# A pause in the weight loads, a later zeroing and a new spacing of transposes in a fused attention and FFN kernel

## The chip, the cores and the metric

One core of a Trainium2 chip. The metric is the device time of one execution in microseconds (us), of which smaller is better. Fast: no more than 1.5% above the fastest of its kernel. "Ratio" is always the mean time of one kernel's fast runs over the mean of the other kernel's fast runs of the same rounds on the same chip, so it is not quite the ratio of the medians quoted beside it. The 95% interval is in brackets.

## The reference

Linear attention with cosine and sine features, followed by a multiplicative feed-forward part, in float32:

```python
# q, k, v: (8 batches, 8 heads, 576 positions, 64)
def phi(x, c, s):
    r = np.maximum(x, 0.0)
    return np.concatenate([r * c, r * s], axis=-1)        # 128 features
q_p, k_p = phi(q, cos_w, sin_w), phi(k, cos_w, sin_w)
kv  = np.einsum('bhsf,bhsd->bhfd', k_p, v)
z   = np.sum(k_p, axis=2)
num = np.einsum('bhsf,bhfd->bhsd', q_p, kv)
den = np.einsum('bhsf,bhf->bhs', q_p, z)[..., None] + 1e-06
x   = (num / den).transpose(0, 2, 1, 3).reshape(4608, 512)
out = ((x @ w1) * (x @ w2) @ w3) @ w_out                   # w1, w2: 512x1024; w3: 1024x1024; w_out: 1024x512
```

## The kernel before

The kernel works on nine tiles of 512 tokens. It multiplies w3 by w_out once (the "w34" work, which needs w3 transposed) and then spends its time in the products with w1, w2 and w34. Attention of the next batches is woven in between: units of work are appended to numbered "slots", and after each group of FFN matmuls the units of its slot are issued, each to its engine's own in-order stream. So the order in a slot list is the order on every engine.

All weights and most inputs are loaded by GpSimd, in one long list that is issued at the start:

```python
for c0, n in ((0, 256), (256, 256), (512, 256), (768, 256)):
    nc.gpsimd.dma_start(out=w1b[:, :, ds(c0, n)], in_=w1v[:, :, ds(c0, n)])
    nc.gpsimd.dma_start(out=w2b[:, :, ds(c0, n)], in_=w2v[:, :, ds(c0, n)])
    if c0 == 256:
        load_first4(nc.gpsimd, q0, q)
nc.gpsimd.dma_start(out=woutb[:], in_=moe_w_out.rearrange("(c p) m -> p c m", p=P))
for jp in range(8):
    load_w3(jp)
    if jp == 4:
        load(1, "k")
load(1, "qv")
load(2, "kqv")
```

The feature buffers exist twice, for even and odd batches. The second set is zeroed by VectorE in mid-kernel:

```python
def feature_buffers(i):
    va = const.tile([P, NCH, H, D + 2], BF16, name=f"va{i}")
    nc.vector.memset(va[:, :, :, D:D + 1], 1.0)
    nc.vector.memset(va[64:128, 4, :, 0:D], 0.0)
    ...                                       # cut: kp and qp, one memset each
```

One chunk of attention is a query transpose (TensorE, then a copy out of PSUM), a numerator (TensorE, then a normalisation on VectorE), and a transpose of the normalised block into xT, the FFN's input:

```python
def q_tr(b, c, evac=True):
    ...                                       # cut: 8 transposes into pst
    on_vector = lambda: nc.vector.tensor_copy(out=dst, in_=src)
    ...
def num(b, c, chain=True):
    nt = ps_att.tile([P, 2, 512], FP32, name="pnum")      # this pool has one buffer
    ...                                       # cut: 8 matmuls, then den, reciprocal, xblk on VectorE
def x_tr(b, c, by_vector=False):
    ...                                       # cut: 4 transposes of xblk into pst
    copy = nc.vector.tensor_copy if by_vector else nc.scalar.copy
    copy(out=xT[t][:, :, ds(o, R)], in_=pst[:, 0:4, 0:R])
```

Where they stand during the first token tile:

```python
slots[6].append(lambda: feature_buffers(1))
slots[6].append(lambda: prep_q(0, 4))
slots[8].append(lambda: q_tr(0, 4))
...
spread(prep_units(1, (prep_k,)), 8, 10, between)
spread(prep_units(1, (prep_q,)), 10, 13, between)
spread(prep_units(1, (prep_v,)), 13, 14, between)
attention_at(1, between, kv=(14, 14, 14, 15, 15), tr=(12, 13, 15, 17, 19),
             nu=(16, 17, 19, 20, 22), xt=(18, 19, 21, 22, 25))
...
spread(prep_units(2, (prep_k,)), 20, 23, slots)   # key features of batch 2: VectorE and ScalarE
```

## Time and profile before

| | before |
|---|---|
| three first runs | 260.17 us median (259.86 to 260.18) |
| span of the profiled execution | 258.3 us |
| TensorE busy | 247.0 us, 96% |
| idle time of TensorE with a named engine behind it | 4.7 us, all before 62 us |

The lines that carry this stand in the prediction below. One more stretch matters for what follows: the end of the first token tile, just before the second tile's first FFN matmul (L428). Timeline columns: start, duration, engine, line, operation, output from input, and in brackets the idle time before it with what ended it.

```profile
63.70 0.59 ACT L369 COPY xT<-pst 128x512 bf16<-128x512 bf16 x1
64.10 0.39 PE L367 MATMUL pst<-identb,xblk 128*128 128x128 bf16 x4
64.17 0.73 ACT L245 ACTIVATE kp<-ks,sinv 128x512 bf16<-128x512 bf16 x1
64.33 0.42 PE L331 MATMUL pnum<-kvs,qpT 128*128 128x65 bf16 x8
64.59 1.02 PE L474 MATMUL ffnps<-w34b,abT 128*128 128x512 bf16 x4
64.80 0.58 ACT L369 COPY xT<-pst 128x512 bf16<-128x512 bf16 x1
65.45 0.81 PE L428 MATMUL ffnps<-xT,w1b 128*128 128x512 bf16 x3
```

Read them engine by engine. ScalarE finishes the last copy into xT at 64.80 + 0.58 = 65.38 us, and TensorE starts the tile that reads it at 65.45: the two are level, TensorE has no idle time there, and its list of waits does not name this place. Nothing stands in reserve either.

### The profile page before, as it was taken

Reading aid. Unit: us, or ns where it says so; the run is one execution under the profiler, and the core shown is the slowest. Engines: PE = TensorE matmul, PEld = TensorE weight load, DVE = VectorE, ACT = ScalarE, POOL = GpSimd, SP = SyncE. Lnnn points to the kernel's source line nnn. Section 1 sums busy time; section 2 is a strip of 40 time slices with the busy share of each in tenths; the row PEclk is TensorE's granted clock in tenths of the full one; section 3 lists DMA queues with packets and bytes.
Section 4 is the critical chain, followed back from the end, with each engine's and each line's share of the span. In section 5 each row is a group of like instructions: output and inputs, shape, how many; then the busy total and the mean of one; then the engine's idle time right before and its main releaser. Section 6 shows DMA issues by size and latency. Waiting matters only on the chain.

```text
span 258.3 us, 5051 instructions
## 1 busy us (share of the span) xinstructions
PE 247.0 (96%) x1934; PEld 134.9 (52%) x1967; DVE 145.6 (56%) x346; ACT 127.9 (49%) x219; POOL 85.6 (33%) x146
## 2 busy tenths in 40 slices
PE   8889899999999999999999999999999999999992
PEld 3478455665565455446454654555455544444441
DVE  6875753856879638833972688178526614303310
ACT  2765224936965555545655465646533233323321
POOL 7854154440670384047305900610140031022000
PEclk9999999999999999999999999999999999999999
DMA  7999999999899599999998999826490252024025
GB/s 191 183 194 202 208 205 201 199 198 199 212 157 146 100 202 175 160 162 176 195 158 173 175 198 133 175 60 122 92 202 13 50 121 76 0 42 122 1 45 120
DMA packets 68025, 37.11 MB, mean 144 GB/s; under 512 B 35616, under 2 KB 64544, under 8 KB 68000
## 3 DMA queue, kind: packets, MB, share of 16 engines
q0 software_dynamic: 35488, 27.20, 65.6%
q1 hardware_dynamic: 32352, 9.44, 22.3%
q8 instruction: 15, 0.25, 0.4%
q10 hardware_dynamic: 160, 0.13, 0.2%
q14 instruction: 10, 0.08, 0.1%
HBM read 38.80 MB, written 9.44 MB: 187 GB/s over the span
## 4 chain that ended last, share of the span: by engine, by line
PE 89%; DMA 3%; DVE 2%; issue 2%; ACT 1%; POOL 1%; ACTq 0%; POOLq 0%
PE ffnps L428 47%; PE ffnps L474 23%; PE ffnps L208 5%; PE pnum L331 4%; PE pst L304 4%; PE pnum L273 3%; DMA qs<-in_q_dram 3%; PE pst L196 1%; PE pst L367 1%; DVE xblk L341 1%; DVE qp L241 0%; POOL vs L120 0%; ACT qpT L307 0%; PE ffnps L491 0%; ACT asb L465 0%
## 5 line engine op out<-in xcount | busy, mean ns | idle before, releaser
L469 DVE TENSOR_TENSOR abT<-asb,ffnps 128x512 bf16<-128x512 bf16 x68 | 46.4, 682 | 65.1 <-PE ffnps L428 64.1
L428 PE MATMUL ffnps<-xT,w1b 128*128 128x512 bf16 (+2 forms) x312 | 74.2, 357 | 0.8 <-DVE xT L369 0.3
L428 PE MATMUL ffnps<-xT,w2b 128*128 128x512 bf16 (+2 forms) x306 | 73.2, 356 | 0.5
L465 ACT CAST asb<-ffnps 128x512 bf16<-128x512 f32 x68 | 39.8, 585 | 63.9 <-PE ffnps L428 56.5
L474 PE MATMUL ffnps<-w34b,abT 128*128 128x512 bf16 x273 | 63.4, 379 | 0.4
L413 POOL DMA_DIRECT2D out_dram<-osb x42 | 22.3, 536 | 121.0 <-ACT osb L480 120.9
L428 PEld LDWEIGHTS <-w1b 128*128 128x128 bf16 x320 | 28.9, 98 | 27.2 <-issue 0.4
L474 PEld LDWEIGHTS <-abT 128*128 128x128 bf16 x280 | 26.5, 98 | 30.1 <-DVE abT L469 0.4
L480 ACT COPY osb<-ffnps 128x512 f32<-128x512 f32 x35 | 20.5, 585 | 38.6 <-PE ffnps L474 37.5
L428 PEld LDWEIGHTS <-w2b 128*128 128x128 bf16 x320 | 27.4, 97 | 22.7
L245 ACT ACTIVATE qp<-qs,sinv 128x512 bf16<-128x512 bf16 (+2 forms) x40 | 28.2, 717 | 1.2 <-DMA qs<-in_q_dram 1.2
L341 DVE TENSOR_TENSOR xblk<-pnum,den 128x512 bf16<-128x512 f32 (+1 forms) x39 | 26.9, 691 | 1.5 <-DVE den L340 0.2
L245 ACT ACTIVATE kp<-ks,sinv 128x512 bf16<-128x512 bf16 (+1 forms) x35 | 24.9, 722 | 0.0
L331 PEld LDWEIGHTS <-qpT 128*128 128x128 bf16 x320 | 15.1, 98 | 9.6 <-DVE xblk L341 1.8
L265 POOL COPY va<-vs 128x512 bf16<-128x512 bf16 (+1 forms) x30 | 18.4, 641 | 0.0
L241 DVE TENSOR_SCALAR qp<-qs,cosv 128x512 bf16<-128x512 bf16 (+1 forms) x40 | 17.9, 454 | 0.6 <-DMA qs<-in_q_dram 0.5
L331 PE MATMUL pnum<-kvs,qpT 128*128 128x65 bf16 x312 | 16.4, 194 | 0.6 <-DVE xblk L341 0.5
L306 DVE COPY qpT<-pst 128x1024 bf16<-128x1024 bf16 (+1 forms) x20 | 12.4, 620 | 7.7 <-PE pst L304 7.5
L273 PEld LDWEIGHTS <-kp 128*128 128x128 bf16 x280 | 12.7, 98 | 5.0
L208 PE MATMUL ffnps<-woutb,w3T 128*128 128x512 bf16 x61 | 15.0, 379 | 0.1
L304 PEld LDWEIGHTS <-qp 128*128 128x128 bf16 x184 | 11.9, 98 | 5.6 <-ACT asb L465 1.1
L304 PE MATMUL pst<-identb,qp 128*128 128x128 bf16 x184 | 13.9, 219 | 0.7 <-ACT asb L465 0.7
(78 smaller groups left out, 178.5 us busy)
## 6 DMA issues: line engine op xcount, KB each, us to landing
out_dram<-osb POOLq DMA_DIRECT2D x16, 256.0 KB, 3.9
out_dram<-osb POOLq DMA_DIRECT2D x24, 128.0 KB, 3.0
qs<-in_q_dram POOLq DMA_DIRECT2D x9, 256.0 KB, 7.9
ks<-in_k_dram POOLq DMA_DIRECT2D x7, 320.0 KB, 7.2
qs<-in_q_dram POOLq DMA_DIRECT2D x7, 320.0 KB, 8.1
vs<-in_v_dram POOLq DMA_DIRECT2D x7, 320.0 KB, 9.6
w3b<-in_moe_w_dram POOLq DMA_DIRECT2D x8, 256.0 KB, 13.6
ks<-in_k_dram POOLq DMA_DIRECT2D x7, 256.0 KB, 7.8
```

Of the source, the lines that this page charges most:

```text
L208: nc.tensor.matmul(acc[:, :], lhsT=w3T[:, lc, :], rhs=woutb[:, lc, :], start=(lc == 0), stop=(lc == 7))
L245: nc.scalar.activation(out=dst[:R, c, 0:n, D:F], in_=src[:R, 0:n, c, :], func=ACTF.Relu, scale=sinv[:R, at:at + 1], bias=0.0)
L273: nc.tensor.matmul(kvt[:, h // 4, ds((h % 4) * 65, 65)], lhsT=kp[:, c, h, :], rhs=va[:, c, h, 0:D + 1], start=(i == 0 and h % 4 == 0), sto ...
L304: nc.tensor.transpose(pst[:, h, :], qp[:, c, h, :], identb[:])
L331: nc.tensor.matmul(nt[:, h // 4, ds((h % 4) * 65, 65)], lhsT=qpT[:, h, ds(at, 128)], rhs=kvs[:, h, :], start=True, stop=True)
L341: nc.vector.tensor_tensor(out=xblk[rows], in0=n4[:, :, :, 0:D], in1=den[rows].unsqueeze(3).to_broadcast([R, 2, 4, D]), op=ALU.mult)
L413: on.dma_start(out=rows[:, :, cols], in_=osb[64 * i:64 * i + rows.shape[0], :, cols])
L428: nc.tensor.matmul(out, lhsT=w[:, kc, ts(jc, 128)], rhs=x[:, kc, tok], start=(kc == 0), stop=(kc == 3))
L465: nc.scalar.copy(out=asb[:], in_=aT[:, :])
L469: nc.vector.tensor_mul(out=abT[:, jc, :], in0=asb[:], in1=bT[:, :])
L474: nc.tensor.matmul(ops[:, :], lhsT=abT[:, jc, ts(ms, 128)], rhs=w34b[:, jc, :], start=(jc == 0), stop=(jc == 7))
L480: nc.scalar.copy(out=osb[:, ms % 2, :], in_=ops[:, :])
```

## The change

Its intent: keep GpSimd's issuing of loads out of the way of VectorE at the start; let the query features of the last chunk of batch 0 run before the zeroing, not after it; and space batch 1's query transposes so that numerators do not queue behind each other's normalisation. The core of the diff (cut: the untouched lines, and the old load list, whose first ten loads stay where they were and whose rest moves into the new function):

```diff
+    def other_loads(behind):
+        seen = sm.tile([P, 1], BF16, name="seen", bufs=1)
+        nc.gpsimd.tensor_copy(out=seen[:], in_=behind)      # waits for the first numerators
+        nc.gpsimd.dma_start(out=w2b[:, :, ds(512, 256)], ...)
+        load_w12(768, 256)
+        ...                                                 # woutb, w3, batches 1 and 2, as before
     num(0, 0)
     q_tr(0, 1, evac=False)[1]()
+    other_loads(att[0]["x"][0][:, 0, 0, 0:1])
-            slots[6].append(lambda: feature_buffers(1))
             slots[6].append(lambda: prep_q(0, 4))
+            slots[11].append(lambda: feature_buffers(1))
-            spread(prep_units(1, (prep_k,)), 8, 10, between)
-            spread(prep_units(1, (prep_q,)), 10, 13, between)
-            spread(prep_units(1, (prep_v,)), 13, 14, between)
-            attention_at(1, between, kv=(14, 14, 14, 15, 15), tr=(12, 13, 15, 17, 19),
-                         nu=(16, 17, 19, 20, 22), xt=(18, 19, 21, 22, 25))
+            spread(prep_units(1, (prep_k,)), 6, 8, between)
+            spread(prep_units(1, (prep_q,)), 10, 12, between)
+            spread(prep_units(1, (prep_v,)), 13, 13, between)
+            attention_at(1, between, kv=(14, 14, 14, 14, 15), tr=(12, 13, 17, 18, 19),
+                         nu=(16, 17, 18, 20, 22), xt=(18, 19, 20, 22, 25))
```

More of the change, by code (lines that the diff above doesn't have):

```diff
@@ L176, with load_w12 @@
     load_first(nc.gpsimd, q0, q, 2, 2)
-    for c0, n in ((0, 256), (256, 256), (512, 256), (768, 256)):
+    def load_w12(c0, n):
         nc.gpsimd.dma_start(out=w1b[:, :, ds(c0, n)], in_=w1v[:, :, ds(c0, n)])
         nc.gpsimd.dma_start(out=w2b[:, :, ds(c0, n)], in_=w2v[:, :, ds(c0, n)])
-        if c0 == 256:
-            load_first4(nc.gpsimd, q0, q)
-    nc.gpsimd.dma_start(out=woutb[:], in_=moe_w_out.rearrange("(c p) m -> p c m", p=P))
-    for jp in range(8):
-        load_w3(jp)
-        if jp == 4:
-            load(1, "k")
-    load(1, "qv")
-    load(2, "kqv")
+    load_w12(0, 256)
+    load_w12(256, 256)
+    load_first4(nc.gpsimd, q0, q)
+    nc.gpsimd.dma_start(out=w1b[:, :, ds(512, 256)], in_=w1v[:, :, ds(512, 256)])
+    def other_loads(behind):
+        seen = sm.tile([P, 1], BF16, name="seen", bufs=1)
+        nc.gpsimd.tensor_copy(out=seen[:], in_=behind)
+        nc.gpsimd.dma_start(out=w2b[:, :, ds(512, 256)], in_=w2v[:, :, ds(512, 256)])
+        load_w12(768, 256)
+        nc.gpsimd.dma_start(out=woutb[:], in_=moe_w_out.rearrange("(c p) m -> p c m", p=P))
+        for jp in range(8):
+            load_w3(jp)
+            if jp == 4:
+                load(1, "k")
+        load(1, "qv")
+        load(2, "kqv")
     w3Ts = {}
```

## The prediction

> **What bounds the kernel now.** I read the page's first part, then the chain of work that ended last, then TensorE's list of waits, and only then the timeline around each wait.
>
> ```profile
> PE 247.0 (96%) x1934; PEld 134.9 (52%) x1967; DVE 145.6 (56%) x346; ACT 127.9 (49%) x219; POOL 85.6 (33%) x146
> PE 89%; DMA 3%; DVE 2%; issue 2%; ACT 1%; POOL 1%; ACTq 0%; POOLq 0%
> ```
>
> TensorE is busy in 96% of a 258.3 us span and carries 89% of the chain. The change leaves the matmuls as they are, so it can only win TensorE's idle time. The list of its waits names all of it that has an engine behind it (columns: us in total, times, longest):
>
> ```profile
> PE unread L168 <- DVE zeros L144: 1.2, 1, 1.2
> PE kva L290 <- DVE va L265: 0.9, 1, 0.9
> PE pst L304 <- ACT asb L465: 0.7, 1, 0.7
> PE pnum L331 <- DVE xblk L341: 0.5, 1, 0.5
> PE pst L367 <- ACT qpT L307: 0.4, 1, 0.4
> PE pst L367 <- DVE xblk L341: 0.3, 1, 0.3
> PE ffnps L428 <- DVE xT L369: 0.3, 1, 0.3
> PE pst L317 <- ACT kvs L296: 0.2, 1, 0.2
> PE pfirst L331 <- DVE qpT L318: 0.2, 1, 0.2
> ```
>
> They sum to 4.7 us, all before 62 us; the first two, 2.1 us, lie before any instruction that the change touches. That leaves 2.6 us, 1.0% of the time: a win of 2% (5.2 us) isn't there to be had.
>
> **What the Trainium skill says.** "SBUF — State Buffer", section "Who interferes with whom": VectorE in a two-port mode and GpSimd share one port pair, an exclusive lock, so the later one blocks fully; copies and tensor_scalar from SBUF to SBUF can enter those modes. "DMA: Bandwidth & Descriptors", section "SWDGE vs HWDGE vs iDMA": GpSimd itself writes the descriptors of its loads into SBUF. Together: a load being issued can stall a VectorE feature instruction. The trace agrees:
>
> ```profile
> 11.21 0.76 POOL L178 DMA_DIRECT2D w1b<-in_moe_w_dram  x1
> 11.44 0.66 DVE L241 TENSOR_SCALAR qp<-qs,cosv 128x512 bf16<-128x512 bf16 x1 [0.49 <-DMA qs<-in_q_dram]
> 11.96 0.76 POOL L179 DMA_DIRECT2D w2b<-in_moe_w_dram  x1
> 12.21 0.62 DVE L241 TENSOR_SCALAR qp<-qs,cosv 128x512 bf16<-128x512 bf16 x1
> 13.41 0.56 DVE L241 TENSOR_SCALAR qp<-qs,cosv 128x512 bf16<-128x512 bf16 x1
> 14.93 0.36 DVE L241 TENSOR_SCALAR qp<-qs,cosv 128x512 bf16<-128x512 bf16 x1
> ```
>
> The same instruction takes 0.34 us at its median over the run (the tile view of qp). Those at 11.44, 12.21 and 13.41 us begin while GpSimd is issuing and end 0.2 to 0.3 us late; the one at 14.93 begins late in an issue and loses nothing. "VectorE: DVE Perf Modes", section "Why PSUM operands drop a tier", says that an operand in PSUM rules the two-port modes out, so the copies from pst and the normalisation from pnum should not care; the xT copy, 0.42 us at 15.81 beside an issue and 0.42 at 17.77 after one, agrees.
>
> **The change, part by part.**
>
> *Loads behind the tenth.* GpSimd copies one column of the first normalised numerators (ready at 15.01 us) before it issues the eleventh load. Before, the eleventh to thirteenth were issued at 11.96, 13.13 and 14.46 us. What this frees is the feature instruction at 12.21: without the issue at 11.96 it takes 0.34 and ends at 12.55, not 12.83. But the next on the path is the copy of the transposed queries (start 12.75), which needs the first half of the transposes: four of the eight from 12.24 on, done about 12.63. So it starts about 12.66, not 12.75: **0.09 us** of the 0.28 reaches the path. The stretch at 13.41 saves 0.2 us that sits beside the transposes and the ScalarE copy at 14.33, so nothing. All TensorE work up to the first FFN matmul (16.29 us) moves by 0.09.
>
> Does the delay make loads late? Each issue in the list reuses the semaphore of the load eight earlier, so GpSimd was throttled by landings anyway: the issues come about 1.33 us apart, as the loads land. At 15 us the sixth to tenth are still in flight; the tenth landed at 20.7. From about 15.2 the new order issues every 0.75 us, and by the w3b load of 18.51 or 20.13 us it has caught up, while transfers still run without a bubble. So I expect the same landings: the eleventh at 22.0 (first used at 27 us), the first w3b at 31.0 (used at 33.4). Cost 0. The added copy is one 128x1 instruction on GpSimd, off the path.
>
> *Zeroing batch 1's buffers later.* Here the trace has:
>
> ```profile
> 24.52 0.69 DVE L453 TENSOR_TENSOR abT<-asb,ffnps 128x512 bf16<-128x512 bf16 x1 [2.08 <-ACT asb L452]
> 25.30 0.09 DVE L150 MEMSET va<- 128x40 bf16 x1
> 25.48 0.27 DVE L151 MEMSET va<- 64x256 uint32 x1
> 25.81 0.48 DVE L155 MEMSET kp<- 64x512 uint32 x1
> 26.35 0.48 DVE L155 MEMSET qp<- 64x512 uint32 x1
> 26.87 0.34 DVE L241 TENSOR_SCALAR qp<-qs,cosv 64x512 bf16<-64x512 bf16 x1
> 27.36 0.61 PE L304 MATMUL pst<-identb,qp 128*128 128x128 bf16 x8 [0.66 <-ACT asb L465]
> ```
>
> The transposes at 27.36 need that qp, done at 27.21. The view puts the wait down to asb because it ended last (27.32), but these transposes don't read asb, and the ScalarE half of qp was done at 25.10; the true releaser is VectorE, kept by 1.5 us of zeroing. In the new order qp comes right behind the product of 24.52, at about 25.25, and is done by 25.6. TensorE's previous matmul started at 26.32 and takes 0.21 at its issue pace (four 512-wide ones in 0.86), so the hole is 27.36 - 26.53 = **0.83 us**, removed whole. The memsets land behind the product that ran at 31.15 to 31.84, where VectorE has 1.13 us idle; 1.5 us there delays the next product by about 0.4 us, and its PSUM tile has two more pairs before reuse. Cost 0.
>
> *Batch 1's query transposes respaced.* The third leaves the gap between the last key-value chunks and the key-value copies; third and fourth move next to the numerators, and one chunk moves ahead of the last w34 matmuls. Now:
>
> ```profile
> 54.63 0.38 ACT L278 CAST kvs<-pnum 128x260 bf16<-128x260 f32 x1 [0.37 <-PE pnum L273]
> 55.04 0.43 DVE L279 CAST kvs<-pnum 128x260 bf16<-128x260 f32 x1 [0.23 <-ACT kvs L278]
> 55.52 0.42 PE L331 MATMUL pnum<-kvs,qpT 128*128 128x65 bf16 x8
> 60.10 0.69 DVE L306 COPY qpT<-pst 128x1024 bf16<-128x1024 bf16 x1 [1.09 <-PE pst L304]
> 61.14 0.69 DVE L341 TENSOR_TENSOR xblk<-pnum,den 128x512 bf16<-128x512 f32 x1
> 61.88 0.43 PE L331 MATMUL pnum<-kvs,qpT 128*128 128x65 bf16 x8 [0.47 <-DVE xblk L341]
> ```
>
> pnum has one buffer, so each numerator waits for the normalisation before it: 0.16 + 0.20 + 0.69 with their starts, about 1.1 us, plus 0.69 if a query copy gets between, as at 60.10. I laid out the new order with these durations, a 0.44 us transpose group, 0.86 us per four FFN matmuls and 0.05 us per handover:
> - The wait at 61.88 (61.03 + 0.21 to 61.88, 0.64 us) goes: two FFN halves' worth of work now stands ahead of that numerator.
> - The wait at 55.52 (0.23 us) grows: ScalarE's last w34 copy (0.58) now lies right ahead of its kvs copy. Last w34 matmul done, 0.58 + 0.38 ScalarE, 0.43 VectorE, 0.05 x 3: first numerator at +1.4, while TensorE has 0.26 + 0.86 of work beyond the 0.17 of drain. About 0.44 us, a loss of 0.21.
> - The numerator of chunk 1 comes sooner after that of chunk 0 and waits about 0.15 us for its normalisation: a loss of 0.15.
> - Small shape switches (64-wide transposes next to FFN matmuls) lose about 0.15 less.
> Sum: 0.64 - 0.21 - 0.15 + 0.15 = **0.42 us** won.
>
> Total: 0.09 + 0.83 + 0.42 = 1.34 us; 260.17 - 1.34 = **258.8 us**. From 65 us on, TensorE's waits in the list are gone, so the shift should be carried to the end unchanged.
>
> **The rivals.**
> 1. *Late loads take the place of the removed waits.* If the pause emptied the transfer queue, all later landings would slip by up to 3.2 us (11.96 to about 15.2), and the w3b transposes, with 2.4 us of slack (1.5 after the gain), would wait: time about 260 to 262. For it: loads are back to back, DMA at 9 tenths until 65 us. Against it: five loads in flight when issuing resumes. I give it one in ten.
> 2. *The respacing gives back as much as it takes.* Numerators, transposes and normalisation share VectorE, and batch 1's values land only at 49.0 us while the new order copies them at about 49.4, not 50.5. If the key-value chunks or the kvs copies wait, the third part is worth 0, or -0.4: 259.3 to 259.6.
> 3. *The lock relief is worth more.* If the whole 0.28 us, or the 0.2 at 13.41 too, reaches the path: 258.4 to 258.6.
>
> **Range and chances.** The three runs before span 0.3 us. The zeroing is the surest term; the respacing may run from -0.2 to +0.8, the start from 0 to 0.4. That gives 258.0 to 259.8 for eight in ten. Faster than 254.97 needs more than all the idle time that the change can reach: 1%. Slower than 265.4 would need a stall that nothing here shows: 1%.
>
> **What would show it.** Right: the wait of 0.7 us at about 27 us missing from TensorE's list; the second query feature of the start at 0.34 to 0.36 us; the first FFN matmul at about 16.2; w3b landings unmoved and no wait for a load; the one-buffer wait near 61 us gone, a slightly longer hole ahead of batch 1's first numerator; about 1.3 us less idle TensorE and unchanged busy time. Wrong: a new wait of w3 transposes or w1b/w2b matmuls for a DMA; the memsets ahead of a product that TensorE then waits for; a numerator wait of 0.5 us or more between 52 and 64 us; a first FFN matmul earlier by 0.3 us or more.

## The result, and the profile after

| | before | after |
|---|---|---|
| six runs each, same rounds | 259.81 us median (259.57 to 260.18) | 258.98 us median (258.70 to 259.12) |
| ratio of the fast runs | | 0.9964 [0.9952, 0.9977] |
| span of the profiled execution | 258.3 us | 257.1 us |

So the change is worth 0.36%, about 0.9 us (0.0036 x 259.8): within 2%, and 258.98 lies inside the predicted range. Line numbers of the changed kernel are 10 higher than those of the kernel before from the loads on. The first part of its page, and TensorE's waits (us in total, times, longest):

```profile
PE 246.4 (96%) x1934; PEld 135.0 (53%) x1967; DVE 145.5 (57%) x346; ACT 128.0 (50%) x219; POOL 85.9 (33%) x147
```

```profile
PE unread L168 <- DVE zeros L144: 1.2, 1, 1.2
PE kva L300 <- DVE va L275: 1.1, 1, 1.1
PE pst L377 <- ACT qpT L317: 0.4, 1, 0.4
PE pst L377 <- DVE xblk L351: 0.4, 1, 0.4
PE pnum L341 <- DVE kvs L289: 0.3, 1, 0.3
PE ffnps L438 <- DVE xT L379: 0.3, 1, 0.3
PE pst L327 <- DVE qp L258: 0.2, 1, 0.2
```

Against the list in the prediction, the wait of 0.7 us put down to `asb` and the wait of 0.5 us of a numerator for `xblk` are gone. A wait of 0.3 us of a numerator for `kvs` is new in the list. No wait is for a DMA. The busy times of TensorE, 247.0 and 246.4 us, cannot be compared so closely: the control in experiment 5, the same code as the kernel before, has 249.3 us, with 33 matmul records more in its trace.

**The zeroing.** These lines are of the changed kernel's timeline:

```profile
24.80 0.34 DVE L251 TENSOR_SCALAR qp<-qs,cosv 64x512 bf16<-64x512 bf16 x1
26.22 0.61 PE L314 MATMUL pst<-identb,qp 128*128 128x128 bf16 x8
26.42 0.58 ACT L475 CAST asb<-ffnps 128x512 bf16<-128x512 f32 x1 [1.15 <-PE ffnps L438]
30.86 0.09 DVE L150 MEMSET va<- 128x40 bf16 x1
31.05 0.27 DVE L151 MEMSET va<- 64x256 uint32 x1
31.37 0.48 DVE L155 MEMSET kp<- 64x512 uint32 x1
31.91 0.48 DVE L155 MEMSET qp<- 64x512 uint32 x1
32.43 0.69 DVE L479 TENSOR_TENSOR abT<-asb,ffnps 128x512 bf16<-128x512 bf16 x1
```

The feature is done at 25.14 us and the transposes at 26.22 no longer have a bracket: they follow the matmuls ahead of them. The copy into `asb` now runs from 26.42 to 27.00, after they have started, so `asb` was not what they had waited for. The memsets fill 30.86 to 32.39 us and hold the product at 32.43 back by 0.60 us, not the 0.4 laid out (it stood at 32.97 before, and TensorE's stream here runs 1.14 us earlier); nothing on TensorE waits for it.

**The spacing.** Two places of the changed kernel's timeline:

```profile
53.27 0.38 ACT L288 CAST kvs<-pnum 128x260 bf16<-128x260 f32 x1
53.68 0.43 DVE L289 CAST kvs<-pnum 128x260 bf16<-128x260 f32 x1 [2.75 <-ACT kvs L288]
54.16 0.42 PE L341 MATMUL pnum<-kvs,qpT 128*128 128x65 bf16 x8 [0.30 <-DVE kvs L289]
...
62.98 0.73 ACT L255 ACTIVATE kp<-ks,sinv 128x512 bf16<-128x512 bf16 x1
...
63.28 0.81 PE L484 MATMUL ffnps<-w34b,abT 128*128 128x512 bf16 x3
...
63.61 0.58 ACT L379 COPY xT<-pst 128x512 bf16<-128x512 bf16 x1
...
64.24 1.02 PE L438 MATMUL ffnps<-xT,w1b 128*128 128x512 bf16 x4
```

The first numerator at 54.16 us has the expected longer hole. The lines from 62.98 us on are the surprise. TensorE's last w34 matmul before the second tile starts at 63.72 us in the records and takes 0.21 at its issue pace, so the next could start at 63.93. It starts at 64.24, 0.31 us later, right behind the xT copy (63.61 + 0.58 = 64.19). That copy stands in ScalarE's stream behind the key feature of batch 2 that runs from 62.98 to 63.71. This wait is not in the list, and the timeline gives it no bracket: idle time is counted from a matmul's modelled end, 63.72 + 0.38 = 64.10, and 0.14 us was left, less than any bracket shows. The chain of work that ended last does name it (start, duration, what):

```profile
62.62 0.48 ACT osb L490
63.09 0.62 ACT kp L255
63.71 0.48 ACT xT L379
64.20 0.04 issue
64.24 1.89 PE ffnps L438 x8
```

The chain runs through ScalarE up to the second tile; in the kernel before it stays on TensorE there. So such a wait is found in the chain, or by hand with the issue pace.

The distance between events of TensorE, from both traces, puts the parts together:

| stretch of TensorE's work | before, us | after, us | gained |
|---|---|---|---|
| start to first FFN matmul | 16.29 | 15.97 | 0.32 |
| from there to the transposes of chunk 4 of batch 0 | 11.07 | 10.25 | 0.82 |
| first w3 transposes to batch 1's numerator of chunk 3 | 30.76 | 30.39 | 0.37 |
| first w3 transposes to the second tile's first FFN matmul | 31.88 | 31.81 | 0.07 |
| start to the second tile's first FFN matmul | 65.45 | 64.24 | 1.21 |

From the second tile on both traces run side by side: the shift is 1.2 us to the last matmul. It is 0.32 + 0.82 + 0.07. The experiments say which of these belongs to the code.

### The profile page after: what moved, and what is told of

It is laid out like the page before. It is cut to its first block, busy times and chain, and to the rows that moved or that the text cites. A ratio compares the mean times of both kernels' runs of the same rounds, so it can differ in the third digit from the quotient of the medians.

```text
span 257.1 us, 5053 instructions
## 1 busy us (share of the span) xinstructions
PE 246.4 (96%) x1934; PEld 135.0 (53%) x1967; DVE 145.5 (57%) x346; ACT 128.0 (50%) x219; POOL 85.9 (33%) x147
## 4 chain that ended last, share of the span: by engine, by line
PE 85%; DMA 7%; ACT 2%; DVE 2%; issue 2%; POOL 1%; ACTq 0%; POOLq 0%
PE ffnps L438 47%; PE ffnps L484 21%; DMA qs<-in_q_dram 7%; PE ffnps L218 4%; PE pnum L341 3%; PE pst L314 3%; PE pnum L283 3%; PE pst L206 1%; ACT kp L255 1%; PE pst L377 1%; DVE va L275 0%; DVE qpT L316 0%; POOL vs L120 0%; ACT qpT L317 0%; PE ffnps L501 0%
## 5 line engine op out<-in xcount | busy, mean ns | idle before, releaser
L283 PE MATMUL pnum<-va,kp 128*128 128x65 bf16 x280 | 14.1, 193 | 0.0
```

Source lines behind the costliest of these rows:

```text
L283: nc.tensor.matmul(kvt[:, h // 4, ds((h % 4) * 65, 65)], lhsT=kp[:, c, h, :], rhs=va[:, c, h, 0:D + 1], start=(i == 0 and h % 4 == 0), sto ...
```

## The experiments

Ten kernels ran, each correct and timed in five rounds against the kernel before.

### 1 to 4: each part alone, and the change without the pause

Four kernels made of the hunks of the diff: `pause_only` has the first two, `zero_only` the move of `feature_buffers(1)`, `space_only` the last hunk, `zero_space` the last two of these together.

> Only the pause of the loads, nothing else of the change. Theory (the lock frees one feature instruction, 0.09 us of it on the path): the second query feature at about 12.2 us takes 0.34 to 0.36 us instead of 0.62, the hole of 0.8 us before the query transposes near 27 us stays, time 0.1 us below before (ratio 0.9996, within noise of 1). Rival (the start really gains the 0.32 us that the trace of the changed kernel shows at its first FFN matmul, 15.97 against 16.29): ratio 0.9988. Rival (late loads): ratio above 1.002 and a TensorE wait for a DMA.

> Only the zeroing moved behind. Theory: the hole of 0.83 us before the transposes near 27 us goes whole, nothing new appears, so -0.8 us, ratio 0.9968. Rival (TensorE really waited for the ScalarE copy asb named in the view): the hole stays and the ratio is 1. Rival (the zeroing costs the same later): a new TensorE wait of some tenths near 32 us, ratio about 0.998.

> Only the respacing. Prediction's sum: -0.42 us. The trace of the changed kernel shows the numerator of chunk 3 earlier by 0.37 us net of the other parts, but then the next token tile's first matmul waits about 0.3 us for ScalarE's copy of xT, held by a key feature of batch 2; so the theory is now -0.1 us, ratio 0.9996, with that new wait in the trace. If the prediction's sum holds to the end: ratio 0.9984.

> The changed kernel without the pause. If the parts add up: 0.8 + 0.1 = -0.9 us, ratio 0.9965, the same as the whole change, which would say that the pause is worth 0.1 us or less. If the pause carries 0.3 us: ratio 0.9976.

| kernel | median, us | before, us | ratio |
|---|---|---|---|
| pause_only | 259.98 | 259.85 | 0.9997 [0.9984, 1.0010] |
| zero_only | 259.03 | 259.85 | 0.9968 [0.9954, 0.9982] |
| space_only | 259.80 | 259.85 | 0.9996 [0.9984, 1.0008] |
| zero_space | 258.90 | 259.85 | 0.9963 [0.9951, 0.9975] |

The product of the three single parts is 0.9961, and the whole change gave 0.9964: the parts add up, and the zeroing carries the gain alone (0.0032 x 259.85 = 0.83 us, with an interval of 0.47 to 1.20). In the timed runs neither of the other two can be told from nothing.

The trace of space_only shows why its part is worth so little. The numerator of chunk 3 comes 30.38 us after the first w3 transposes, against 30.76 before: 0.38 us are won there. The second tile's first FFN matmul comes after 31.82 us, against 31.88. So 0.31 us is given back in the last microsecond, in the same wait as in the whole change.

The trace of pause_only reaches its first FFN matmul at 15.84 us. But without the pause zero_only has 16.06 there, space_only 15.97 and zero_space 16.26, so this trace by itself says nothing on the pause.

### 5: the kernel before, once more

The same code as the kernel before, run as if it were a change.

> The kernel before, unchanged, as a control. Ratio 1 within 0.001. Its trace is a second draw of the start: theory (which of VectorE and GpSimd takes the shared port first changes from run to run without any change of code): the first FFN matmul anywhere between 15.8 and 16.3 us, the holes at 27 us (0.83) and 61 us (0.64) the same as in the first trace.

Measured: 259.74 us, ratio 0.9997 [0.9984, 1.0011]. Its first FFN matmul starts at 15.85 us, 0.44 us earlier than in the first trace of the same code. So the 0.32 us at the start in the table above lies inside what one code does from run to run. As expected, both holes are the same as in the first trace: from the first FFN matmul to the transposes of chunk 4 it takes 11.07 us again, and 30.77 us (30.76) from the first w3 transposes to the numerator of chunk 3. Of the 0.44 us, 0.15 comes from the first load of q, which landed at 11.26 and not at 11.41, and 0.30 from the first query feature, which took 0.35 us and not 0.66 as at 11.44 in the prediction's lines. The second query feature, at about 12 us, which took 0.62 us in the first trace, took 0.35 here and 0.35 in zero_only and space_only, all without the pause, and 0.63 in zero_space. In the three traces where it was not held, GpSimd's issue near 11.7 us was instead: it took 0.85 us, not 0.74 to 0.76.

### 6: the tenth load behind the wait as well

```diff
-    nc.gpsimd.dma_start(out=w1b[:, :, ds(512, 256)], in_=w1v[:, :, ds(512, 256)])
     def other_loads(behind):
         ...
-        nc.gpsimd.dma_start(out=w2b[:, :, ds(512, 256)], in_=w2v[:, :, ds(512, 256)])
+        load_w12(512, 256)
```

> The whole change, with the tenth load behind the wait as well. It takes away the issue at 10.5 to 12 us that can hold the first query feature (0.66 us against 0.35). Theory: only in executions where the lock falls that way is there something to win, so at most 0.3 us and on average 0.1: ratio 0.9960 to 0.9964. Rival (the issues matter more than that): 0.9950 or less. The four loads in flight at 15 us still keep the queue busy, so no later landing.

Measured: 259.09 us against 260.12, ratio 0.9964 [0.9951, 0.9976], the same as the change. No gain is seen; an interval of 0.33 us to each side leaves the expected 0.1 open. The tenth load, issued at 15.23 us and not at 10.49, landed at 20.57 (20.96 in the changed kernel), so this wait has not yet cost anything.

### 7: a longer pause

The pause is real in its means but idle in effect. Is it harmless at any length? Here the eleventh load waits for the numerators of chunk 3, ready at about 21.8 us, not for those of chunk 0 at 14.7.

```diff
-    other_loads(att[0]["x"][0][:, 0, 0, 0:1])
...
             slots[3].append(lambda: num(0, 3))
+            slots[3].append(lambda: other_loads(att[0]["x"][3][:, 0, 0, 0:1]))
```

> The whole change, but the eleventh load waits for the fourth numerators (chunk 3, ready at about 21.5 us) instead of the first (14.7 us). Theory of the prediction (the pause is free because five loads are in flight when issuing resumes): now the tenth has landed at about 20.8 us before the eleventh is issued, the queue runs dry for about 3 us, all later landings slip by about 2.5 to 3 us, and the w3 transposes or the FFN matmuls wait for loads: ratio 0.9964 plus about 0.004 to 0.01. If the loads had more slack than the trace says: ratio stays at 0.9964.

Measured: 265.74 us against 260.12, ratio 1.0221 [1.0207, 1.0235]. The direction was as expected, the size far more. Busy time by stretch, first of the changed kernel, then of this one. The columns after the window and its length are busy us and instructions of PE, PEld, DVE, ACT and POOL, then TensorE's granted clock, the DMA share and GB/s:

```profile
20.00:22.00 2.00, 1.65 (x26) 1.30 (x24) 1.72 (x5) 1.07 (x2) 1.37 (x3) 1.00 1.45 197
22.00:24.00 2.00, 2.00 (x36) 1.97 (x34) 0.12 (x1) 1.00 (x2) 0.63 (x2) 1.00 1.40 200
```

```profile
20.00:22.00 2.00, 1.65 (x25) 1.30 (x23) 1.71 (x5) 1.07 (x2) 0.16 (x1) 1.00 0.01 1
22.00:24.00 2.00, 2.00 (x38) 1.99 (x36) 0.37 (x1) 0.76 (x2) 1.96 (x4) 1.00 0.26 15
...
32.50:36.88 4.38, 0.34 (x2) 0.00 (x1) 0.76 (x2) 0.59 (x1) 0.56 (x1) 0.88 1.18 206
36.88:42.80 5.92, 5.92 (x27) 3.24 (x28) 2.07 (x3) 0.00 (x0) 3.13 (x5) 0.51 1.19 204
42.80:48.00 5.20, 5.20 (x44) 3.06 (x43) 1.38 (x2) 1.43 (x3) 2.15 (x5) 1.00 1.21 207
```

In the change the transfers go on at 197 and 200 GB/s. With the long pause the queue runs empty: 1 and 15 GB/s. The first w3 landing moves from 31.27 to 36.84 us, and the w3 transposes wait for it:

```profile
PE pst L206 <- DMA w3b<-in_moe_w_dram: 4.0, 1, 4.0
...
36.88 1.04 PE L206 MATMUL pst<-identb,w3b 128*128 128x128 bf16 x8 [4.04 <-DMA w3b<-in_moe_w_dram]
```

Now the clock column: 0.51 from 36.88 to 42.80 us. The Trainium skill, "TensorE: Matmul & The Clock Gate", section "HAM oscillation — how this bites in real kernels", gives the rule "no PE-idle gaps >~3.4µs", after which the next matmuls run at half rate. The trace agrees: the gap is 4.2 us (32.67 to 36.88; the clock record falls to half at 35.86 and returns to full at 42.69), and behind it 512-column matmuls start 0.43 us apart, not 0.215. The first to the third group of w3 transposes take 6.31 us, against 3.48 in the changed kernel, so the slow clock costs 2.83 us more. Start later by 0.25, wait 4.21, slow clock 2.83: 7.29 us, and the second tile starts 7.29 us later than in the changed kernel. The wait itself came out longer than expected, and this second cost was not expected at all.

So the first rival of the prediction is real, only not at this length of pause. Between 14.7 and 21.8 us the pause turns from free to 7 us; at what length, no run here shows.

### 8: the new wait taken away

If the wait at 64.24 us is what eats the gain of the spacing, taking that xT copy off ScalarE should win it back. VectorE is made to do this one copy:

```diff
-                slots[xt[i]].append(lambda c=c: x_tr(b, c))
+                slots[xt[i]].append(lambda c=c: x_tr(b, c, by_vector=(b == 1 and c == 2)))
```

> The whole change, and VectorE instead of ScalarE copies chunk 2 of batch 1's xT. Theory: the wait of 0.31 us at about 64.2 us is for that copy, which ScalarE takes only after a key feature of batch 2; so it goes, and the ratio falls from 0.9964 by 0.0012 to 0.9952. Rival (the wait only moves on, as VectorE is then late with the next normalisation): ratio 0.9964 and a wait at the next transposes.

Measured: 261.06 us against 260.12, ratio 1.0043 [1.0030, 1.0055]. The expectation failed in size and sign. Yet the wait did go: from the first w3 transposes to the second tile it takes 31.51 us, against 31.81. The loss is elsewhere, and the tail of the timeline of xt_vector shows it:

```profile
250.52 0.59 ACT L490 COPY osb<-ffnps 128x512 f32<-128x512 f32 x1 [1.14 <-PE ffnps L484]
251.40 0.37 ACT L503 COPY osb<-ffnps 128x256 f32<-128x256 f32 x1 [0.29 <-PE ffnps L501]
251.80 2.84 ACTq L423 DMA_DIRECT2D out_dram<-osb  x1
254.68 0.37 ACT L503 COPY osb<-ffnps 128x256 f32<-128x256 f32 x1 [2.91 <-issue]
255.08 0.50 ACTq L423 DMA_DIRECT2D out_dram<-osb  x1
```

The same of the changed kernel:

```profile
250.57 0.59 ACT L490 COPY osb<-ffnps 128x512 f32<-128x512 f32 x1 [1.14 <-PE ffnps L484]
251.45 0.37 ACT L503 COPY osb<-ffnps 128x256 f32<-128x256 f32 x1 [0.29 <-PE ffnps L501]
251.85 0.56 ACTq L423 DMA_DIRECT2D out_dram<-osb  x1
252.45 0.37 ACT L503 COPY osb<-ffnps 128x256 f32<-128x256 f32 x1 [0.63 <-PE ffnps L501]
252.85 0.48 ACTq L423 DMA_DIRECT2D out_dram<-osb  x1
```

Until 251.4 us xt_vector is level with the changed kernel, 0.05 us ahead, although it began 0.25 us later. Then ScalarE's first DMA issue of the tail takes 2.84 us, not 0.56, and holds the last output copy back by 2.23 us. The bracket `<-issue` says that the profile knows nothing the engine waited for. The page lists a DMA queue of the kind "instruction" (q14) with only ten packets; its last packets before the end of the span are, from the raw records:

| kernel | ScalarE instructions | last packet but one, us | last, us | first tail issue of ScalarE |
|---|---|---|---|---|
| changed kernel | 219 | 241.35 | 250.30 | at 251.85, 0.56 us |
| xt_vector | 218 | 241.27 | 252.98 | at 251.80, 2.84 us |

The last packet falls into the stalled issue. In the other eleven traces it comes 1.54 to 1.60 us ahead of that issue; here it was missing at that place, before the stall began, so the stall did not make it late. That suggested a theory: taking one instruction out of ScalarE's stream moved the point where its next instructions have to be fetched, so that ScalarE came to it while issuing that DMA. The rival theory was that VectorE's copy upset the tail in some other way.

### 9 and 10: the same copy, with the instruction count restored

`xt_pad` is xt_vector with one more tiny activation on ScalarE at the very start, where ScalarE is idle. `after_pad` is the changed kernel with the same addition.

```diff
-    nc.scalar.activation(out=tiny[:], in_=zeros[:, 0:1], func=ACTF.Relu, scale=1.0, bias=0.0)
+    nc.scalar.activation(out=tiny[:], ...); nc.scalar.activation(out=tiny[:], ...)   # the same, twice
```

> The kernel of xt_vector with one more 128x1 activation on ScalarE at the very start, where ScalarE is idle; nothing else differs. Fetch theory: xt_vector lost 2.3 us only because taking one instruction out of ScalarE's stream moved a fetch of its instructions onto its first output copy of the tail; with the count restored, that issue takes 0.5 to 0.6 us again instead of 2.84, the last packet of the instruction queue comes back to about 250.3 us, and the ratio to the kernel before is 0.995 to 0.9955, faster than the changed kernel by about 0.3 us. Rival (VectorE's copy of the chunk is itself the cause, through the order of the two engines in the tail): the issue stays at 2.8 us and the ratio at 1.004.

> The changed kernel with the same extra activation. Fetch theory: one more instruction ahead moves the fetches relative to the work the other way, so the last packet of the instruction queue comes a little earlier than at 250.3 us and the tail stays as it is: ratio 0.996 to 0.997, first output copy of ScalarE issued in 0.5 to 0.6 us. Rival (any change of the count upsets the tail, or the extra instruction costs something at the start): the issue takes 2 us or more, ratio 1.003 or above; or the first FFN matmul is later than 16.3 us.

| kernel | median, us | before, us | ratio | last q14 packet, us | first tail issue |
|---|---|---|---|---|---|
| xt_pad | 258.80 | 259.98 | 0.9952 [0.9940, 0.9965] | 249.97 | 0.56 us |
| after_pad | 259.08 | 259.98 | 0.9962 [0.9949, 0.9976] | 250.35 | 0.56 us |

The times, the issues and xt_pad's packet came as the fetch theory said. after_pad's packet was also to come a little earlier than at 250.30 us; it came at 250.35, or 0.04 us earlier when counted back from the issue, which is within what the other traces scatter. So that a count one higher moves the fetch is not shown. An instruction that does no useful work, placed 250 us ahead of the stall, took the stall away: 261.06 became 258.80 us. VectorE's copy is the same in xt_vector and in xt_pad, so it is not the cause. That the queue q14 feeds ScalarE, and so that the stall is a wait for instructions, is inferred from this, not labelled in the trace. Why the fetch came too late in one case and not in the other stays open: only 218 instructions stalled, 219 (changed kernel and xt_pad) and 220 (after_pad) did not.

In xt_pad the second tile looks like this:

```profile
62.97 1.34 ACT L255 ACTIVATE kp<-ks,sinv 128x512 bf16<-128x512 bf16 x2
62.99 0.42 DVE L379 COPY xT<-pst 128x512 bf16<-128x512 bf16 x1
...
63.91 0.81 PE L438 MATMUL ffnps<-xT,w1b 128*128 128x512 bf16 x3
```

VectorE's copy is done at 63.41 us, beside the key features on ScalarE, and the tile starts at 63.91, one issue pace after the last w34 matmul. The first FFN matmul of the kernel was at 15.95 us (15.97 in the changed kernel), so these two traces compare directly: 64.24 to 63.91 at the second tile, and 257.08 to 256.76 at the end. Of the 0.33 us at the second tile 0.02 is the earlier start and 0.30 the new wait, which is gone (from the first w3 transposes 31.51 us, not 31.81). In the timed runs it is the fastest kernel and beats the kernel before clearly; against the change its interval overlaps, so that step rests on the traces.

## Why the prediction was right or wrong

**The time.** Predicted 258.8 us, measured 258.98. The change gains about 0.9 us, not 1.34. It comes near in part because 260.17, the median of three runs from which the prediction subtracted, was a little high: later rounds put the kernel before at 259.74 to 260.12. Taken from the 259.81 of the same rounds, 1.34 would have given 258.47, half a microsecond too low. The chances were right too: with only 2.6 us of removable idle time, 2% was not there.

**The zeroing: right in mechanism and size.** 0.83 us predicted, 0.82 in the trace, 0.83 in the timed run of that part alone (interval 0.47 to 1.20). Two readings held: that the view named the wrong releaser, and that the memsets would be hidden where they were moved to, though they hold the next product back by 0.60 us, not 0.4.

**The pause: right only for one state of the start.** The prediction took the feature of 0.62 us at 12.21 us for a property of the kernel. In the five traces without the pause, 0.62 or 0.63 us was seen twice, 0.35 three times; with the pause it was 0.34 to 0.35 each time. So the pause does remove the stall, but the stall was there only sometimes. Its ratio of 0.9997 has an interval of about 0.13% to each side, 0.34 us: too wide for 0.09 us. The traces are finer. In nine of the twelve the first query feature took 0.35 us, and the first FFN matmul came 4.55 to 4.56 us after that feature's start, also in zero_space, where the second feature was held (0.63 us): there the stall cost nothing. In the first trace of the kernel before, the first feature was held as well (0.66 us), and it was 4.85 us. pause_late had its first feature held just as long and its second free:

```profile
11.43 0.66 DVE L251 TENSOR_SCALAR qp<-qs,cosv 128x512 bf16<-128x512 bf16 x1 [0.49 <-DMA qs<-in_q_dram]
...
12.20 0.34 DVE L251 TENSOR_SCALAR qp<-qs,cosv 128x512 bf16<-128x512 bf16 x1
12.66 0.42 DVE L328 COPY qpT<-pst 128x512 bf16<-128x512 bf16 x1
```

The copy of the transposed queries starts at 12.66 us, not 12.75, as the prediction had worked out, and the first FFN matmul comes after 4.79 us. So the pause is worth about 0.06 us where the first feature is held too, and nothing was seen elsewhere; that rests on one pair of traces. The start scatters for other reasons, 15.84 to 16.22 us with the pause and 15.85 to 16.29 without: the first load of q lands between 11.26 and 11.68 us, and the first feature is sometimes held. The prediction also named "a first FFN matmul earlier by 0.3 us or more" as a sign against it. The trace of the changed kernel has just that (0.32), and the control shows it to be scatter.

**No late loads: right for this pause.** The tenth load landed at 20.96 us (20.71 before), the eleventh at 22.28 (22.03), the first w3 at 31.27 (31.01): about 0.25 later each, far inside the slack, and without the pause the control's first w3 landed at 31.22 too. That the transfers ran without a bubble was the reason given, and the long pause shows what happens with one.

**The spacing: the step that failed.** Up to the numerator of chunk 3 it is 0.37 us against 0.42 predicted, with the wait at 61.9 gone and the hole at the first numerator grown from 0.23 to 0.46, as laid out. What failed is the last sentence of the sum: "From 65 us on, TensorE's waits in the list are gone, so the shift should be carried to the end unchanged." The layout ended at the numerators, and the list of waits was taken for a list of what can wait. At the second tile's first matmul the kernel before had no wait, but no slack either: the copy it needs ended 0.07 us before it started. With TensorE 0.4 us earlier, and that copy still behind a key feature on ScalarE, a new wait of 0.31 us took its place. The spacing was worth 0.07 us in this trace. Taking the wait away in xt_pad brought 0.30 us back.

**The rivals.** The second, "the respacing gives back as much as it takes", is what happened, but by another way than the one named: not the values' landing or the kvs copies, but a copy of ScalarE after them. Its time of 259.3 to 259.6 was too high because of the base: 0.09 + 0.83 taken from 259.81 is 258.89, and 258.98 was measured. The third did not happen: the two held features together cost the start 0.30 us, but the change frees only the second.

## What to carry to other kernels

A gain at one place reaches the end only through every later meeting of engines, so after removing a wait, lay out the new order to the next place where the critical engine needs another's result, and compare ends and starts there even where no wait is listed; the chain of work that ended last shows where it leaves the critical engine. Trace the unchanged kernel twice before explaining any difference of a few tenths of a microsecond: here one code scattered by 0.44 us at its start, and counting from the event that set the start showed what the times could not. And when a small change costs more than its own work could, compare the traces to the very end for something unrelated to its work; where an instruction fetch is suspected, adding a dummy instruction far ahead is a cheap test.

## What the Trainium skill lacked or had wrong

- "SBUF — State Buffer", "Who interferes with whom": it says that whoever issues first gets the shared ports and the other blocks, but not that this order can change between runs of the same code. Here the same feature instruction took 0.62 us in one trace and 0.35 in the next, where GpSimd's issue beside it took 0.85 us, not 0.76.
- "Runtime: NRT & Kernel Launch", "Instruction fetch mechanics": it tells that a sequencer fetches its next instructions through a DMA queue of its own while it runs, mostly hidden, and names a taken branch as what stalls it. It does not tell of a stall like the one inferred here: a DMA issue of ScalarE took 2.84 us, not 0.56, with the late packet of an instruction queue (252.98 us) inside it, in a kernel with one ScalarE instruction fewer, and not when that count was restored.
